# Filler matmuls that read the constant identity, with another set of the planner's numbers, in an attention and feed-forward kernel

## Chip, cores and metric

The kernel runs on one core of a Trainium2 chip. The metric is the device time in microseconds, the median of the runs shown; a lower time is better. Engines are named as in the profile: PE (TensorE) with PEld for its weight loads, DVE (VectorE), ACT (ScalarE), POOL (GpSimd), and SP, which issues most of the transfers.

## What is computed

For 4 batches and 8 heads with 576 positions of width 64, the reference computes causal softmax attention and a linear memory read, mixes them per head, and puts the result through a feed-forward layer:

```python
scores = np.where(causal, -1e9, scale * q @ k.T)
local = softmax(scores) @ v
mem_out = (phi(q) @ M_prev) / (phi(q) @ z_prev + 1e-6)   # phi(x) = (x if x > 0 else exp(x) - 1) + 1
x = g * mem_out + (1 - g) * local                        # g = sigmoid(beta), per head
r = np.maximum(x @ w_in, 0.0)                            # 2304 x 512 by 512 x 2048
out = (s * r * r + b) @ w_out                            # 2304 x 2048 by 2048 x 512
```

Both weights come as 64-bit floats and are converted on the chip.

## The kernel before

The work has two phases. The first, up to some 300 us, holds the attention of 16 pairs of heads (g = 0 to 15, pair p of batch b), the conversion of w_in, and the first feed-forward product for all rows of the first two batches and part of the third. The second holds the rest of that product, the conversion of w_out and the second product.

A pair goes through these steps. PE computes scores from qk into two PSUM tiles sb (L383). DVE adds the mask and takes the row minimum of the negated scores (L390) into P, which frees sb. ACT takes the exponential with row sums (L396). DVE turns the sums into 1/sum (L435, L436), and DVE or POOL scales P (L402). Beside this the memory part runs: a max (L319 on ACT, L321 on DVE or L323 on POOL), an exponential (L324), L325 on DVE, a product with z (L329), a sum (L331), L332 and a reciprocal (L335) on DVE, and a product that is put beside the scores in P (L342). PE transposes P in four groups, which the code calls banks, against the constant ident into four PSUM tiles tb (L463). ACT or DVE copies them out, to pt (L472) and F (L474, L476, L479). PE multiplies them with V, which holds v and the memory matrix (L514). The result is split into a high and a low part: ACT copies the high part (L535) and DVE subtracts (L536) into xs or x4, which gives the PSUM tile back.

The conversion of w_in goes in 20 pieces. Each piece uses one raw buffer xa of three and one work buffer of two, w0 and w1 (WT in the code). ACT starts it (L560), three DVE steps follow on the same buffer (L561, L562, L564), then the high part is made on ACT or POOL (L569, L567) and the low part on DVE or POOL (L571, L573). The first product (L580 to L582) takes xs or x4 and both parts.

No scheduler of the framework orders the first phase. The class `Plan` (L44) holds every step with an engine, an estimated cost, a rank, what it reads and writes, and which PSUM tile it takes and gives back. Its function `deal` places the steps in time by these estimates, lowest rank first among those that can go, and the program is written out in that order. Semaphores are put in from what each instruction really reads and writes. The tables from L292 on are its inputs: per pair, which engine takes the max (RELU), the copies (COPY, one letter for each of four banks) and the scalings (SCAL, one letter for each of five row blocks), when a pair is due (AT), and offsets for ranks (UC for copies, UX for the splits, RPS and RQS for the memory part). HIGH and LOW give the engine for the two parts of each piece of w_in.

After all steps are placed, `waits` (L157) goes over PE's steps. Where the plan shows PE idle for longer than two fillers and a margin, and a PSUM tile is free over that gap, it puts in filler matmuls. They are written by `warm`: 128 columns of `busy` against themselves. `busy` is no constant: it is the first 128 columns of the work buffer w0, cleared once at the start.

```python
busy = WT[0][:, :128]                                                        # L268
plan.idle = "TS", 0.3, lambda n, pool, k: warm(n, TB[k] if pool == "T" else SB[k])   # L291
raw, w = RAWS[n % 3][:, :n_], WT[n % 2][:, :n_]                              # L547
```

Of the kernel before, what the change touches and what calls it, by code (L numbers as in the profile page):

```python
# [43 lines left out]
class Plan:  # L44
# [6 lines left out]
    RATE = 220.0e3  # L51
    SWITCH = {"full": 0.22, "row": 0.13, "col": 0.13}
    TURN = 110
    HOLD, WORK, WAIT = (2.5, 3), (1, 5), (0.15, 0.05)
    FREE = {"DVE": 0.05, "POOL": 0.10}

    def __init__(self, **pools):
# [4 lines left out]
    def add(self, eng, cost, fn, rank, reads=(), writes=(), take=(), give=(), bytes=0, mode=None, slack=0.0, port=False):  # L62
        s = dict(eng=eng, cost=cost, fn=fn, rank=rank, take=take, give=give, bytes=bytes, mode=mode, slack=slack, port=port or eng == "POOL",
                 n=len(self.steps), out=[], end=None)
        deps = {self.wrote[k]["n"]: self.wrote[k] for k in (*reads, *writes) if k in self.wrote}
        for k in writes:
            deps |= {r["n"]: r for r in self.read.pop(k, ())}
            self.wrote[k] = s
        for k in reads:
            self.read.setdefault(k, []).append(s)  # L70
        s["need"] = len(deps)
        s["deps"] = list(deps.values())
        for d in s["deps"]:
            d["out"].append(s)
        self.steps.append(s)
        return s
# [95 lines left out]
def attention_moe_kernel(  # L172
# [15 lines left out]
    nc = tc.nc  # L188
# [16 lines left out]
    ident = const.tile([128, 128], F32, name="ident")  # L205
# [36 lines left out]
    SB = [ps_a.tile([128, 1024], F32, name=f"sb{k}") for k in range(2)]  # L242
    TB = [ps_a.tile([128, 512], F32, name=f"tb{k}") for k in range(4)]
# [23 lines left out]

    busy = WT[0][:, :128]  # L268

    def warm(n, ps):  # L270
        for _ in range(n):
            nc.tensor.matmul(ps[:, :128], lhsT=busy, rhs=busy, start=True, stop=True)

    def setup():
        nc.vector.memset(busy, 0.0)
        nc.vector.memset(omg, 0.0)
        warm(WARM, TB[3])
        nc.gpsimd.memset(mask, 0.0)
        for r, c in ((slice(0, 128), slice(448, 576)), (slice(0, 64), slice(576, 640)), (slice(64, 128), slice(576, 640))):
            nc.gpsimd.affine_select(  # L280
                out=mask[r, c], in_=mask[r, c], pattern=[[-1, c.stop - c.start]],
                compare_op=ALU.is_ge, fill=NEG, base=0, channel_multiplier=1,
            )
        for t in SM:
            nc.gpsimd.memset(t, 1e-9)
# [2 lines left out]
    same = lambda x: x  # L288

    plan = Plan(S=2, T=4)  # L290
    plan.idle = "TS", 0.3, lambda n, pool, k: warm(n, TB[k] if pool == "T" else SB[k])  # L291
    WARM, FILL = 7, (0, 0, 0, 0)  # L292
    UR, UC, UX = 1.5, 2, 1
    RP, RC, RT, RA, RX = 0.7, 0.5, 1.4, 2.0, 2.6
    RPS = [0.6, 0.9, -0.5, 0.6, 0.6, 0.6, 0.2, 0.6, ] + [-2] * 8
    RQS = [0, -1.5, 0.5, -1, 0.9, -1, 0.7, 0.3, ] + [0.9] * 8
    RSR, WL = 0.6, 5
    RELU = "APAAADPAADAAAAAA"
    ZMUL = "PPPDDDDDDPPPPPPP"
    PUTS = "PPPDPPPPDDPPPPPP"  # L300
    COPY = ["AADD", "DAAD", "AAAD", "AAAA", "AAAA", "AAAA", "AAAA", "AAAD", "DDAD", "AAAD", ] + ["AAAD"] * 6
    SCAL = ["PPPPP", "PPPPP", "DPPPP", "DDDDD", "DPPPP", "PPPDD", "DPPPD", "DDDDD", "DPPPD", "PPPDD", ] + ["PPPPP"] * 6
    HIGH, LOW = "AAPAAAAAPPAAAPAPPPAA", "DPPDDPDPDDPDDDDDPDDD"
    PARTS = "3232332223222222"
    AT = [-1.4, 0.9, 5.1, 7.8, 12.2, 13.1, 15.5, 19.7, 24.3, 26.2, 29.8, 31.5, 47.5, 23.2, 53.5, 29.1]
    W0, W1, W2, W3, WA, WB, WC, WD, WS = 4.5, 6.3, 6, 4, 8, 10, 14, 0.4, 0.6

    def phi(g):
        b, p = divmod(g, NP)
        u, r0 = g % 2, AT[g]  # L310
        q, z, n, P = QS_[u], ZS[u], NRM[u], PR[u]
# [5 lines left out]
            writes=[("z", u)], bytes=65536)  # L317
        if RELU[g] == "A":
            add("ACT", 0.72, lambda: nc.scalar.activation(PHR, q, AF.Relu), r0 + RPS[g], [("q", u)], ["phr"])  # L319
        elif RELU[g] == "D":  # L320
            add("DVE", 0.45, lambda: nc.vector.tensor_scalar(PHR, q, 0.0, None, ALU.max), r0 + RPS[g], [("q", u)], ["phr"], port=True)  # L321
        else:
            add("POOL", 0.88, lambda: nc.gpsimd.tensor_scalar(PHR, q, 0.0, None, ALU.max), r0 + RPS[g], [("q", u)], ["phr"])  # L323
        add("ACT", 0.72, lambda: nc.scalar.activation(q, q, AF.Exp), r0 + RPS[g] + 0.01, [], [("q", u)])  # L324
        add("DVE", 0.73, lambda: nc.vector.scalar_tensor_tensor(q, q, 1.0, PHR, ALU.min, ALU.add), r0 + RPS[g] + 0.1,  # L325
            ["phr"], [("q", u)], port=True)
        side = lambda c: (("POOL", nc.gpsimd), ("DVE", nc.vector))[c == "D"]
        ez, mul = side(ZMUL[g])
        add(ez, 1.54 if ez == "POOL" else 0.83, lambda: mul.tensor_mul(  # L329
            PHR, q, z.unsqueeze(1).to_broadcast([128, 5, 2, D])), r0 + RQS[g] + 0.01, [("q", u), ("z", u)], ["phr"], port=True)  # L330
        add("DVE", 0.73, lambda: nc.vector.tensor_reduce(n, PHR, AX.X, ALU.add), r0 + RQS[g] + 0.02, ["phr"], [("n", u)])  # L331
        add("DVE", 0.08, lambda: nc.vector.scalar_tensor_tensor(  # L332
            n, n, 1e-6, gin[:, hp:hp + 2].unsqueeze(1).unsqueeze(3).to_broadcast([128, 5, 2, 1]), ALU.add, ALU.mult),
            r0 + RQS[g] + 0.03, ["gin"], [("n", u)], port=True)
        add("DVE", 0.13, lambda: nc.vector.reciprocal(n, n), r0 + RQS[g] + 0.04, [], [("n", u)])  # L335

# [17 lines left out]
    def attention(g):  # L354
        b, p = divmod(g, NP)
        u, r0 = g % 2, AT[g]
        own = g >= NP
# [48 lines left out]
        for v, group in enumerate(visits):  # L406
# [60 lines left out]
        def copy(put, k, h, ps):  # L467
            t = TB[ps[h]]
            hs = slice(64 * h, 64 * h + 64)
            half = lambda a: a.rearrange("p j (r c) -> p j r c", c=128)[:, :, :, hs]  # L470
            if k < 2:
                put(pt[:, :, :, 128 * k:128 * k + 128][:, :, :, hs], t.rearrange("p (j r c) -> p j r c", j=2, c=64))  # L472
            elif k == 2:
                put(half(F[:, :, 320:832]), t.rearrange("p (j r c) -> p j r c", j=2, c=64))  # L474
            elif h:
                put(F[:, :, 0:384].rearrange("p j (r c) -> p j r c", c=128)[:, :, :, 0:64],  # L476
                    t[:, 0:384].rearrange("p (j r c) -> p j r c", j=2, c=64))
            else:
                put(half(F[:, :, 64:320]), t[:, 0:256].rearrange("p (j r c) -> p j r c", j=2, c=64))  # L479

        join = JOIN[g]
        some = [((0, 3),) if join in "ac" else ((0,), (3,)), ((1, 2),) if join in "bc" else ((1,), (2,))]
# [8 lines left out]
        for q, k in enumerate((0, 3, 1, 2)):  # L491
            ps = PS[k]
            r = r0 + RT + 0.1 * q
            for h in range(2):
                cost = dict(A=0.48 if k < 3 else 0.30 + 0.13 * h, D=0.58 if k < 3 else 0.33 + 0.13 * h)
                c = COPY[g][k]
                add(dict(A="ACT", D="DVE")[c], cost[c], lambda k=k, h=h, ps=ps: copy(
                    dict(A=nc.scalar.copy, D=nc.vector.tensor_copy)[COPY[g][k]], k, h, ps), r + 0.1 - UC,
                    [("tp", g, k)], [("pt", u if k > 1 else 2, h, k)], give=[(ps, h, "T")])
# [90 lines left out]
    def first(m, b, f, EARLY):  # L590
        ps = []
        pool = HOME[m]
        part = lambda: TB[ps[0]] if pool == "T" else SB[ps[0]][:, :CM]
# [28 lines left out]
            tick()  # L622

    LEFT = 7
    HOME = "TTTTTTTTTSTTTTTTTTTTTSSSSSTTSSSTSTTSSSTSS"
    JOIN = "b0b00000b0caa0bb"
    EARLY = 1
    MM = [(b, f) for b in range(B - 1) for f in range(NF - LEFT * (b == 2))]
    WRANK = [W0, W1, W2, W3] + [WA + WD * k for k in range(4)] + [WB + WD * k for k in range(4)] + [
# [259 lines left out]
    for t in range(NPT):  # L889
        if t == 0:  # L890
            g_load(1)
        for i, m in enumerate(SEQ):
            n = 7 * t + i + AH
# [3 lines left out]
            n = i if t else i - 2  # L897
# [55 lines left out]
```

## Time and profile before

| | before |
|---|---|
| runs | 556.72, 556.23, 555.96 us, median 556.23 |
| profiled execution | 556.89 us, span 555.1 us |
| PE busy | 540.1 us, 97% of the span |
| DVE, ACT, POOL busy | 398.4, 400.6, 258.2 us |
| granted clock, mean | 0.991 |
| chain that ended last | PE 89%, DVE 6%, ACT 3%, POOL 1% |
| calls of the filler | 39, seven of them at the very start |

The span is 1.8 us shorter than the time of the same execution, and that execution is 0.66 us above the median. PE is nearly always busy and holds most of the chain, so the places to read are those where it is not: the page's slices show PE under nine tenths in the first seventy microseconds, and a granted clock of six tenths in one of them. A call of the filler on 32-bit data is two records in the trace. Idle time in front of a group stands with what ended it, and the chain tells whether that wait mattered for the end.

### The profile page before, as it was taken

What the parts mean: (1) busy time and instruction counts of PE and PEld (TensorE: products, weight loads), DVE (VectorE), ACT (ScalarE), POOL (GpSimd) and SP (SyncE); (2) the same over time, 40 slices, a digit from 0 to 9 for tenths busy, and PEclk for the clock granted to TensorE, in tenths of its full rate; (3) what the DMA queues carried; (4) which work ended last, traced back from release to release, by engine and by line L of the source; (5) the groups of instructions that cost most, each with busy time, mean ns of one, the idle gap of its engine ahead of it and who ended that gap; (6) DMA issues with size and microseconds to landing.
All of it is one profiled execution on the core that took longest, in us unless ns stands there. A gap on an engine that the chain in (4) does not pass through costs nothing.

```text
span 555.1 us, 11449 instructions
## 1 busy us (share of the span) xinstructions
PE 540.1 (97%) x4086; PEld 445.9 (80%) x4086; DVE 398.4 (72%) x976; ACT 400.6 (72%) x878; POOL 258.2 (47%) x273
## 2 busy tenths in 40 slices
PE   8988799999999999999999999999999999999997
PEld 6756577777777777777778888889999999999996
DVE  5998799999896643324219969334888898888872
ACT  6887789876688963666435668959987977987840
POOL 4971256331445861442400000327578669668760
PEclk9999699999999999999999999999999999999999
DMA  6645566735535443221157564538425435353101
GB/s 198 182 141 176 156 204 213 243 125 159 178 108 162 123 127 122 78 86 63 58 180 312 190 239 157 190 125 289 142 87 155 140 112 165 105 153 122 39 30 38
DMA packets 56665, 81.50 MB, mean 147 GB/s; under 512 B 7584, under 2 KB 39072, under 8 KB 56608
## 3 DMA queue, kind: packets, MB, share of 16 engines
q1 hardware_dynamic: 54064, 78.63, 44.0%
q10 hardware_dynamic: 2544, 2.14, 1.1%
q8 instruction: 32, 0.52, 0.4%
q14 instruction: 25, 0.20, 0.1%
HBM read 57.15 MB, written 23.59 MB: 145 GB/s over the span
## 4 chain that ended last, share of the span: by engine, by line
PE 89%; DVE 6%; ACT 3%; POOL 1%; issue 1%; DVEq 0%; ACTq 0%; POOLq 0%
PE yps L808 12%; PE yps L812 11%; PE sb L514 7%; PE sb L383 6%; PE hps L580 5%; PE hps L581 5%; PE hps L582 5%; PE tb L580 5%; PE yps L811 5%; PE yps L810 5%; PE tb L463 4%; PE tb L581 4%; PE tb L582 4%; PE sb L580 3%; PE sb L582 2%; PE sb L581 2%
## 5 line engine op out<-in xcount | busy, mean ns | idle before, releaser
L396 ACT ACTIVATE P<-P,mn 128x448 f32<-128x448 f32 (+4 forms) x160 | 88.4, 561 | 25.9 <-DVE mn L390 24.8
L402 POOL TENSOR_SCALAR P<-P,sr,omg 128x192 f32<-128x192 f32 (+4 forms) x120 | 76.5, 654 | 64.9 <-DVE sr L436 45.2
L812 PE MATMUL yps<-rb,op 128*128 128x256 f32 x360 | 101.1, 281 | 0.0
L390 DVE CUSTOM_DVE_ANT_0 P<-sb,mask 128x448 f32<-128x448 f32 (+4 forms) x160 | 70.8, 481 | 21.7 <-PE sb L383 21.5
L808 PE MATMUL yps<-rb,op 128*128 128x512 f32 x216 | 76.9, 396 | 0.0
L812 PEld LDWEIGHTS yps<-rb,op 128*128 128x128 f32 x360 | 67.9, 189 | 0.0
L383 PE MATMUL sb<-qk 64*128 64x288 f32 (+4 forms) x384 | 58.5, 420 | 1.1 <-DVE mn L390 0.8
L788 POOL TENSOR_TENSOR sum<-src 128x512 f32<-128x512 f32 x10 | 13.0, 1298 | 90.9 <-ACT src L772 76.2
L796 POOL TENSOR_TENSOR op<-src,op 128x512 fp32r<-128x512 f32 x30 | 43.8, 1480 | 20.0 <-ACT op L795 19.9
L819 DVE TENSOR_TENSOR yu<-yu,yps 128x256 f32<-128x256 f32 x90 | 36.5, 413 | 20.1 <-PE yps L812 19.1
L383 PEld LDWEIGHTS sb<-qk 64*128 64x128 f32 x384 | 36.4, 194 | 15.4 <-issue 5.3
L463 PEld LDWEIGHTS tb<-ident,P 64*128 64x128 f32 x928 | 36.7, 142 | 14.3 <-issue 4.2
L808 PEld LDWEIGHTS yps<-rb,op 128*128 128x128 f32 x216 | 40.6, 188 | 9.0
L463 PE MATMUL tb<-ident,P 64*128 64x64 f32 x928 | 41.2, 230 | 5.5 <-DVE P L402 2.4
L810 PE MATMUL yps<-rb,op 128*128 128x256 f32 x144 | 40.5, 281 | 0.0
L811 PE MATMUL yps<-rb,op 128*128 128x256 f32 x144 | 40.5, 281 | 0.0
L795 ACT CAST op<-src 128x512 fp32r<-128x512 f32 x50 | 30.4, 615 | 12.1 <-PE yps L812 10.6
L796 DVE TENSOR_TENSOR op<-sum,op 128x512 fp32r<-128x512 f32 x36 | 38.8, 1078 | 0.2
L472 ACT COPY pt<-tb 128x512 f32<-128x512 f32 x58 | 31.1, 588 | 9.9 <-PE tb L463 5.2
L796 POOL TENSOR_TENSOR op<-w1H,op 128x512 fp32r<-128x512 f32 x24 | 35.0, 1483 | 0.0
L587 ACT ACTIVATE r<-hps 128x256 f32<-128x256 f32 x62 | 21.9, 382 | 16.3 <-DMA r_d<-r 12.1
L396 ACT ACTIVATION_READ_ACCUMULATOR P<-P,mn 128x1 f32 x160 | 31.5, 197 | 0.0
(172 smaller groups left out, 1549.7 us busy)
## 6 DMA issues: line engine op xcount, KB each, us to landing
r_d<-r SPq DMA_DIRECT2D x41, 256.0 KB, 2.3
src<-r_d SPq DMA_DIRECT2D x20, 512.0 KB, 4.7
qk<-in_qk_t_dram SPq DMA_DIRECT2D x15, 576.0 KB, 4.3
raw<-in_moe_w_out_dram SPq DMA_DIRECT2D x16, 512.0 KB, 7.1
w1H<-r_d SPq DMA_DIRECT2D x16, 512.0 KB, 4.4
xa<-in_moe_w_in_dram SPq DMA_DIRECT2D x12, 512.0 KB, 4.4
r_d<-r SPq DMA_DIRECT2D x48, 128.0 KB, 1.8
qs<-in_q_rows_dram SPq DMA_DIRECT2D x16, 320.0 KB, 4.0
```

The source lines that it names most:

```text
L383: nc.tensor.matmul(at(ps, j, o, n), lhsT=qk[rs, 128 * i:128 * i + 128], rhs=qk[rs, S + 64 + c0:S + 64 + c0 + n], start=True, stop=True, ti ...
L390: nc.vector.tensor_tensor_reduce(P[:, j, PB[i] + 64:PB[i] + 64 + n], at(ps, j, o, n), m, -SCALE, 3.0e38, ALU.add, ALU.min, mn[:, j, i:i + 1])
L396: nc.scalar.activation(pt, pt, AF.Exp, scale=-1.0, bias=mn[:, j, i:i + 1], accum_out=sm[:, j, i, 0:1])
L402: e.tensor_scalar(pt, pt, sr[:, j, i:i + 1], omg[:, h:h + 1], ALU.mult, ALU.mult)
L463: nc.tensor.transpose(TB[ps[h]][:, o[h]:o[h] + 64], P[rs, j, c:c + 128], ident[rs, rs], tile_position=(64 * h, 0))
L580: nc.tensor.matmul(ps, lhsT=wH[:, p, fs], rhs=xs[:, 0], start=p == 0, stop=False)
L581: nc.tensor.matmul(ps, lhsT=wH[:, p, fs], rhs=xs[:, 1], start=False, stop=False)
L796: (nc.gpsimd if m in ONPOOL else nc.vector).tensor_sub(L, x, H.bitcast(F32))
L808: nc.tensor.matmul(tile, lhsT=H, rhs=B, start=f == 0, stop=False)
L810: nc.tensor.matmul(ps, lhsT=H, rhs=B[:, 0], start=f == 0, stop=False)
L811: nc.tensor.matmul(ps, lhsT=H, rhs=B[:, 1], start=False, stop=False)
L812: nc.tensor.matmul(ps, lhsT=L, rhs=B[:, 0], start=False, stop=f == KF - 1)
```

## The change

The fillers that `waits` puts in read `ident` where they read `busy`; the seven at the start keep `busy`. With that come other values in the planner's tables: the margin for staying in a PE mode, UC, UX, RT, RA, RPS, RQS, WL, RELU, COPY, SCAL, HIGH, LOW, AT, W3, HOME and JOIN. Nothing that is computed changes.

```diff
@@ class Plan
-    HOLD, WORK, WAIT = (2.5, 3), (1, 5), (0.15, 0.05)
+    HOLD, WORK, WAIT = (2.5, 3), (1, 5), (0.05, 0.05)
@@ fillers
-    def warm(n, ps):
+    def warm(n, ps, some=busy):
         for _ in range(n):
-            nc.tensor.matmul(ps[:, :128], lhsT=busy, rhs=busy, start=True, stop=True)
+            nc.tensor.matmul(ps[:, :128], lhsT=some, rhs=some, start=True, stop=True)
...
-    plan.idle = "TS", 0.3, lambda n, pool, k: warm(n, TB[k] if pool == "T" else SB[k])
+    plan.idle = "TS", 0.3, lambda n, pool, k: warm(n, TB[k] if pool == "T" else SB[k], ident)
...
-    UR, UC, UX = 1.5, 2, 1
-    RP, RC, RT, RA, RX = 0.7, 0.5, 1.4, 2.0, 2.6
+    UR, UC, UX = 1.5, 1, 2
+    RP, RC, RT, RA, RX = 0.7, 0.5, 1.2, 2.6, 2.6
...
-    RELU = "APAAADPAADAAAAAA"
+    RELU = "AAPAADPAADAAAAAA"
...
-    COPY = ["AADD", "DAAD", "AAAD", "AAAA", "AAAA", "AAAA", "AAAA", "AAAD", "DDAD", "AAAD", ] + ["AAAD"] * 6
-    SCAL = ["PPPPP", "PPPPP", "DPPPP", "DDDDD", "DPPPP", "PPPDD", "DPPPD", "DDDDD", "DPPPD", "PPPDD", ] + ["PPPPP"] * 6
-    HIGH, LOW = "AAPAAAAAPPAAAPAPPPAA", "DPPDDPDPDDPDDDDDPDDD"
+    COPY = ["ADAD", "DAAD", "AAAD", "AAAA", "AAAA", "AAAA", "AAAA", "AAAD", "DDAD", "DAAD", ] + ["AAAD"] * 6
+    SCAL = ["PPPPP", "PPPPP", "DPPPP", "DDDDD", "DPPPP", "PPPDD", "PPPDD", "DDDDD", "PPPDD", "PPDDD", ] + ["PPPPP"] * 6
+    HIGH, LOW = "AAPAPAAAPPAAPPAAPAPA", "DPPDDPDPDDPDDDDDDPDP"
...
-    AT = [-1.4, 0.9, 5.1, 7.8, 12.2, 13.1, 15.5, 19.7, 24.3, 26.2, 29.8, 31.5, 47.5, 23.2, 53.5, 29.1]
+    AT = [0.6, 1.5, 4.8, 7.8, 11.7, 13.1, 15.5, 20.1, 24.5, 26.2, 31.1, 32.1, 47.5, 27.5, 54.0, 32.0]
...
```

The order on DVE in the middle of the conversion of the third piece of w_in (w0) and the fourth (w1), with the splits of pair 2 between; in brackets which engine or queue each waits for. Before:

```order
L562 SCALAR_TENSOR_TENSOR w0_106<-xa1_104,w0_106 128x256 [waits DMAHW4_49,DVE_49]
L562 SCALAR_TENSOR_TENSOR w1_107<-xa2_105,w1_107 128x256 [waits DMAHW3_49,DVE_49]
L536 TENSOR_TENSOR x4_141<-tb1_99,x4_141 128x64 [waits PE_49,Activation_49]
L564 SCALAR_TENSOR_TENSOR w0_106<-xa1_104,w0_106 128x256 [waits DVE_49,PE_49]
L536 TENSOR_TENSOR xs_135<-tb1_99,xs_135 128x256
```

and with the change:

```order
L562 SCALAR_TENSOR_TENSOR w0_106<-xa1_104,w0_106 128x256 [waits DMAHW4_49,DVE_49]
L562 SCALAR_TENSOR_TENSOR w1_107<-xa2_105,w1_107 128x256 [waits DMAHW3_49,DVE_49]
L536 TENSOR_TENSOR x4_141<-tb2_100,x4_141 128x64 [waits PE_49,Activation_49]
L564 SCALAR_TENSOR_TENSOR w0_106<-xa1_104,w0_106 128x256 [waits DVE_49]
L536 TENSOR_TENSOR xs_135<-tb2_100,xs_135 128x256
```

The steps stand in the same order; L564 no longer waits for PE.

The same place on PE: the end of the product with V of pair 2, the fillers, the first transposes of pair 3. Before:

```order
L514 MATMUL tb3_101<-F0_127,V0_125 64x256 x2
L514 MATMUL tb3_101<-pt_129,V0_125 64x256 x6
L514 MATMUL tb3_101<-F0_127,V0_125 64x128 x2
L272 MATMUL tb2_100<-w0_106 128x128 [waits DVE_49]
L272 MATMUL tb2_100<-w0_106 128x128 x7
L463 MATMUL tb2_100<-ident_65,P1_124 128x64
```

and with the change:

```order
L514 MATMUL tb1_99<-F0_127,V0_125 64x256 x2
L514 MATMUL tb1_99<-pt_129,V0_125 64x256 x6
L514 MATMUL tb1_99<-F0_127,V0_125 64x128 x2
L272 MATMUL tb3_101<-ident_65 128x128 x8
L463 MATMUL tb3_101<-ident_65,P1_124 128x64 [waits DVE_49]
```

The eight fillers stay where they were and wait for nothing; the wait for DVE stands at the first transpose.

DVE between the last reductions of pair 1 (P1) and the first of pair 2 (P0, sb1). Before:

```order
L435 TENSOR_REDUCE sr1_122<-sm1_120 128x2x4 [waits Activation_49]
L325 SCALAR_TENSOR_TENSOR qs1_114<-qs1_114,phr_108 128x640 [waits Activation_49]
L436 RECIPROCAL sr1_122<-sr1_122 128x2x4 [waits DVE_49]
L474 COPY F0_127<-tb0_98 128x2x4x64 [waits PE_49]
L474 COPY F0_127<-tb1_99 128x2x4x64 [waits PE_49]
L435 TENSOR_REDUCE sr1_122<-sm1_120 128x2 [waits Activation_49]
L436 RECIPROCAL sr1_122<-sr1_122 128x2 [waits DVE_49]
L479 COPY F0_127<-tb0_98 128x2x2x64 [waits PE_49]
L476 COPY F0_127<-tb2_100 128x2x3x64 [waits PE_49,Activation_49]
L331 TENSOR_REDUCE nrm1_116<-phr_108 128x10 [waits Pool_49]
L390 ISA P0_123,mn0_117<-sb1_97,mask_102 128x448 [waits PE_49]
```

and with the change:

```order
L479 COPY F0_127<-tb2_100 128x2x2x64 [waits PE_49]
L476 COPY F0_127<-tb3_101 128x2x3x64 [waits PE_49]
L435 TENSOR_REDUCE sr1_122<-sm1_120 128x2x4 [waits Activation_49]
L436 RECIPROCAL sr1_122<-sr1_122 128x2x4 [waits DVE_49]
L435 TENSOR_REDUCE sr1_122<-sm1_120 128x2 [waits Activation_49]
L436 RECIPROCAL sr1_122<-sr1_122 128x2 [waits DVE_49]
L472 COPY pt_129<-tb0_98 128x8x64 [waits PE_49]
L472 COPY pt_129<-tb1_99 128x8x64 [waits PE_49]
L325 SCALAR_TENSOR_TENSOR qs1_114<-qs1_114,phr_108 128x640 [waits Activation_49]
L390 ISA P0_123,mn0_117<-sb1_97,mask_102 128x448 [waits PE_49]
```

L325 has moved behind the copies, the two L474 have gone to ACT and two L472 have come, and L331 has moved further down. Later on DVE, L335 of pair 1 stood ahead of the first L561 and now stands right behind it. On POOL the two L342 of pair 0 have moved ahead of its two 576-wide L402, and five L402 of pair 1 ahead of its L329.

## Rows read from the trace of the kernel before

**Rows 1.** Busy time of each engine in four stages, with granted clock and DMA share.

```profile
10.00:34.00 24.00, 21.32 (x238) 15.54 (x237) 22.68 (x76) 20.06 (x61) 20.49 (x27) 1.00 0.62 193
52.00:68.00 16.00, 11.49 (x98) 8.86 (x100) 11.43 (x40) 9.45 (x27) 3.28 (x4) 0.68 0.50 158
68.00:140.00 72.00, 72.00 (x606) 54.25 (x604) 70.71 (x202) 59.66 (x153) 28.42 (x35) 1.00 0.58 186
140.00:230.00 90.00, 89.68 (x775) 68.03 (x772) 53.12 (x186) 63.26 (x171) 48.52 (x67) 1.00 0.41 131
```

The columns are the stretch and its length, then PE, PEld, DVE, ACT and POOL busy with their records, the granted clock, DMA share, GB/s.

**Rows 2.** Chain that ended last, 51 to 55 us: start, length, what.

```profile
52.32 2.07 PE tb L272 x16
...
54.41 0.43 DVE w L564
```

**Rows 3.** Timeline of DVE, 52 to 64 us: start, length, instruction, idle before.

```profile
52.52 0.22 DVE L536 TENSOR_TENSOR x<-tb,x 128x64 fp32r<-128x64 f32 x1
54.41 0.43 DVE L564 SCALAR_TENSOR_TENSOR w<-xa,w 128x256 uint32<-128x256 uint32 x1 [1.68 <-PE tb L272]
...
60.68 0.29 DVE L561 TENSOR_SCALAR w<-w 128x256 uint32<-128x256 uint32 x1 [1.07 <-PE tb L272]
...
63.34 0.35 DVE L390 CUSTOM_DVE_ANT_0 P<-sb,mask 128x192 f32<-128x192 f32 x1
```

**Rows 4.** Timeline of PE, 58 to 67 us.

```profile
58.55 0.87 PE L463 MATMUL tb<-ident,P 64*128 64x64 f32 x10 [1.76 <-DVE P L402]
...
64.79 2.24 PE L383 MATMUL sb<-qk 64*128 64x288 f32 x8
66.95 0.83 PE L514 MATMUL tb<-F,V 128*64 128x320 f32 x4
```

**Rows 5.** Timeline of DVE, 17 to 41 us.

```profile
17.14 0.22 DVE L335 RECIPROCAL nrm<-nrm 128x10 f32<-128x10 f32 x1
...
19.67 1.24 DVE L325 SCALAR_TENSOR_TENSOR qs<-qs,phr 128x640 f32<-128x640 f32 x1 [0.33 <-ACT qs L324]
...
23.15 0.81 DVE L331 TENSOR_REDUCE nrm<-phr 128x10 f32<-128x640 f32 x1
...
27.07 2.10 DVE L561 TENSOR_SCALAR w<-w 128x256 uint32<-128x256 uint32 x1
...
40.35 0.28 DVE L561 TENSOR_SCALAR w<-w 128x256 uint32<-128x256 uint32 x1
```

**Rows 6.** Timeline of POOL, 15 to 36 us.

```profile
15.46 1.63 POOL L402 TENSOR_SCALAR P<-P,sr,omg 128x576 f32<-128x576 f32 x2
...
18.83 1.41 POOL L342 TENSOR_TENSOR P<-qs,nrm 128x384 f32<-128x384 f32 x2
...
22.52 5.12 POOL L402 TENSOR_SCALAR P<-P,sr,omg 128x448 f32<-128x448 f32 x9
27.61 1.41 POOL L342 TENSOR_TENSOR P<-qs,nrm 128x384 f32<-128x384 f32 x2
...
34.45 1.68 POOL L329 TENSOR_TENSOR phr<-qs,z 128x640 f32<-128x640 f32 x1 [3.20 <-DVE qs L325]
```

**Rows 7.** Groups of DVE's instructions by shape, 66 to 230 us: busy, mean ns, idle before.

```profile
L402 DVE TENSOR_SCALAR P<-P,sr,omg 128x448 f32<-128x448 f32 x6 | 4.3, 722 | 0.0
L402 DVE TENSOR_SCALAR P<-P,sr,omg 128x64 f32<-128x64 f32 x8 | 2.6, 351 | 0.0
L472 DVE COPY pt<-tb 128x512 f32<-128x512 f32 x4 | 2.5, 675 | 0.0
L402 DVE TENSOR_SCALAR P<-P,sr,omg 128x320 f32<-128x320 f32 x2 | 1.4, 722 | 0.0
```

**Rows 8.** Busy time by engine, 57 to 67 us (columns as in rows 1).

```profile
57.00:67.00 10.00, 7.31 (x60) 5.58 (x60) 7.17 (x27) 7.11 (x19) 2.09 (x3) 0.50 0.47 153
```

**Rows 9.** Timelines of DVE and of PE, 112 to 117 us.

```profile
112.77 1.65 DVE L402 TENSOR_SCALAR P<-P,sr,omg 128x576 f32<-128x576 f32 x2
...
116.48 0.71 PE L463 MATMUL tb<-ident,P 64*128 64x64 f32 x16
```

More of the change, by code (lines that the diff above doesn't have):

```diff
@@ L290, in attention_moe_kernel @@
     plan = Plan(S=2, T=4)
-    plan.idle = "TS", 0.3, lambda n, pool, k: warm(n, TB[k] if pool == "T" else SB[k])
+    plan.idle = "TS", 0.3, lambda n, pool, k: warm(n, TB[k] if pool == "T" else SB[k], ident)
     WARM, FILL = 7, (0, 0, 0, 0)
-    UR, UC, UX = 1.5, 2, 1
-    RP, RC, RT, RA, RX = 0.7, 0.5, 1.4, 2.0, 2.6
-    RPS = [0.6, 0.9, -0.5, 0.6, 0.6, 0.6, 0.2, 0.6, ] + [-2] * 8
-    RQS = [0, -1.5, 0.5, -1, 0.9, -1, 0.7, 0.3, ] + [0.9] * 8
-    RSR, WL = 0.6, 5
-    RELU = "APAAADPAADAAAAAA"
+    UR, UC, UX = 1.5, 1, 2
+    RP, RC, RT, RA, RX = 0.7, 0.5, 1.2, 2.6, 2.6
+    RPS = [0.6, 0.9, 0, 0.6, 0.6, 0.6, 0, 0.4, ] + [-2] * 8
+    RQS = [0.7, -1, 0.9, -1, 0.9, 0.5, 0.5, 0, ] + [0.7] * 8
+    RSR, WL = 0.6, 3
+    RELU = "AAPAADPAADAAAAAA"
     ZMUL = "PPPDDDDDDPPPPPPP"
     PUTS = "PPPDPPPPDDPPPPPP"
-    COPY = ["AADD", "DAAD", "AAAD", "AAAA", "AAAA", "AAAA", "AAAA", "AAAD", "DDAD", "AAAD", ] + ["AAAD"] * 6
-    SCAL = ["PPPPP", "PPPPP", "DPPPP", "DDDDD", "DPPPP", "PPPDD", "DPPPD", "DDDDD", "DPPPD", "PPPDD", ] + ["PPPPP"] * 6
-    HIGH, LOW = "AAPAAAAAPPAAAPAPPPAA", "DPPDDPDPDDPDDDDDPDDD"
+    COPY = ["ADAD", "DAAD", "AAAD", "AAAA", "AAAA", "AAAA", "AAAA", "AAAD", "DDAD", "DAAD", ] + ["AAAD"] * 6
+    SCAL = ["PPPPP", "PPPPP", "DPPPP", "DDDDD", "DPPPP", "PPPDD", "PPPDD", "DDDDD", "PPPDD", "PPDDD", ] + ["PPPPP"] * 6
+    HIGH, LOW = "AAPAPAAAPPAAPPAAPAPA", "DPPDDPDPDDPDDDDDDPDP"
     PARTS = "3232332223222222"
-    AT = [-1.4, 0.9, 5.1, 7.8, 12.2, 13.1, 15.5, 19.7, 24.3, 26.2, 29.8, 31.5, 47.5, 23.2, 53.5, 29.1]
-    W0, W1, W2, W3, WA, WB, WC, WD, WS = 4.5, 6.3, 6, 4, 8, 10, 14, 0.4, 0.6
+    AT = [0.6, 1.5, 4.8, 7.8, 11.7, 13.1, 15.5, 20.1, 24.5, 26.2, 31.1, 32.1, 47.5, 27.5, 54.0, 32.0]
+    W0, W1, W2, W3, WA, WB, WC, WD, WS = 4.5, 6.3, 6, 5, 8, 10, 14, 0.4, 0.6
     def phi(g):
@@ L624, in attention_moe_kernel @@
     LEFT = 7
-    HOME = "TTTTTTTTTSTTTTTTTTTTTSSSSSTTSSSTSTTSSSTSS"
-    JOIN = "b0b00000b0caa0bb"
+    HOME = "TTTTTTTTTSTTTTTTTTTTTSTSSSTTSSSTSTTSSSTSS"
+    JOIN = "b0b00000b000a0bb"
     EARLY = 1
```

## The prediction

> **What bounds the kernel now.** I read the table by stage first, for one question: in which stages is TensorE (PE) not full. From 68 us to 230 it is busy 72.00 of 72 us and 89.68 of 90, and VectorE (DVE) beside it 70.71 of 72 in the first of these [rows 1]. So from 68 us on the time is a fixed amount of PE work, and an edit pays only by letting that dense part begin earlier, or costs by tearing it open. The stages that are not full are 10 to 34 us (21.32 of 24) and above all 52 to 68 us (11.49 of 16), where the mean granted clock is 0.68 as well [rows 1].
>
> Then I read what ends the waits in 52 to 68. The chain that ended last shows a piece that computes nothing: 16 records of the filler line L272, 2.07 us, between two DVE steps on the conversion buffer w [rows 2]. In DVE's timeline the second of these, L564, sits idle 1.68 us until PE's L272 is done; 6 us later L561 waits 1.07 us for the same reason [rows 3]. That is a knot: the fillers read w0, so they wait for the step that writes it, and the next step on w0 waits for the fillers, with DVE's whole queue behind it: the xs copies that give PSUM back, and the scalings L402 that the next transposes need.
>
> **The change part by part.**
>
> *The fillers read the identity.* The order on both engines shows L564 without its wait on PE, at the same place, and the eight fillers without a wait. L564 then follows the L536 before it (52.52 and 0.22 [rows 3]) at about 52.7 us instead of 54.41; everything from L571 to the last L402 moves up with it, and so do the transposes at 58.55 us [rows 4]. That is **-1.7 us** on the path. The fillers themselves start when the PV product ends and use time in which PE has nothing else. The 1.07 us at L561 I cost at nothing: the scores of 64.79 us wait for PE's own transposes and fillers, while DVE had finished the last reduction that gives their PSUM back at about 63.7 us (63.34 and 0.35) [rows 3, 4]. If PE gets over 1.1 us faster there, that cover is gone and the 1.07 us counts too.
>
> *Fewer fillers.* 39 calls become 35, two records each: 8 records at about 0.13 us (2.07 over 16 [rows 2]) make 1.0 us less PE work, all of it in waits that end with another engine: 0. Bounds: 0 and -1.0.
>
> *The new order between 17 and 34 us.* In the old order DVE's L325 of pair g=1 starts at 19.67 us, and the plain shift L561 takes 2.10 us at 27.07, against 0.28 for the same shape at 40.35 [rows 5]. During those 2 us POOL runs the end of L402 and both L342 [rows 6], so 1.8 us is blocking, not work. In the new order L325 stands behind the copies F and two L472 of pair 0. Walk: L335 ends at 17.4 us [rows 5]; POOL now runs the L342 pair (1.41) ahead of the two 576-wide L402 (1.63) [rows 6], so these end near 20.3; the transposes that need them give the first L472 at about 21.0, L325 ends at 23.1 with both copies before it (0.675 each [rows 7]) and its own 0.8, or at 23.5 if POOL blocks it as at 19.67. That is 2.2 to 2.6 us later than before (19.67 and 1.24). POOL fills the gap with five of the nine L402 that made 5.12 us (some 2.9 us) [rows 6], so the L342 pair of g=1 starts near 27.9 instead of 27.61. From the L331 at 23.15 to L561 DVE needs 3.9 us [rows 5], and the same steps now follow L325, so it comes to L561 near 27.2; L335, for which that L342 pair waits, now stands behind L561, so POOL itself has to stop and let it through: it ends near 28.2 instead of 29.1, and 0.2 goes to L335. Taken: **-0.7 us**, passed on because DVE is nearly full until 52 us. Bounds: -1.8, if nothing blocks L561; +2.6, if POOL does idle in front of the late L329. I take a value near the first since POOL's work is moved, not added: the max of pair 2 (L323), which it gets in place of pair 1's, falls before the 3.20 us in which it idled until 34.45 [rows 6].
>
> The Trainium skill, SBUF — State Buffer, section Who interferes with whom, says that VectorE and GpSimd hold a shared pair of ports as an exclusive lock for one instruction at a time. By that L561 should have lost only the rest of one L402, some 0.5 us; here it lost 1.8 over three POOL instructions, so the trace is harsher than the page [rows 5, 6]. Going by the page for the new order, L561 loses less still and the term would be about -1.1; the total would move by 0.4 us.
>
> *The clock.* The granted clock is 0.50 from 57 to 67 us, with 7.31 us of PE work in it [rows 8]; before it fell PE had run only the fillers, then transposes with idle time between. That pattern stays. Bounds: the fall does not come, half of 7.31, -3.7; the clock rises at the same moment as now, and the PV product that began at 66.95 us [rows 4] slides 2.4 us into the slow part and returns half of that, +1.2. With the low-work part shifted whole, I take 0.
>
> *After 68 us.* Tables for later pairs give DVE four L402 of 448, two of 320 and two L472 more, and four L402 of 64 less: 4 x 0.722 + 2 x 0.722 + 2 x 0.675 - 4 x 0.351 = 4.3 us [rows 7]; one L571 leaves for POOL, uncounted. Of these only the pair for g=6 (two times 0.37) lies in 68 to 140, where DVE has 1.3 us free; the rest falls after 140, where it is busy 53.12 of 90 [rows 1]. PE is not waiting at the closest place I found: L402 ends at 114.4 and its transposes run at 116.48 [rows 9]. Taken: 0. If the cover is gone: 4.3 - 1.3 = +3.0.
>
> Sum: -1.7 - 0.7 = -2.4. On the profiled execution (556.89 us, span 555.1) that is 554.5; the median of the runs is 0.66 lower, so the median becomes **553.8 us**.
>
> **The rivals.**
>
> *No slow clock.* The stretch is shorter by 1.7 us and PE idles less in it, so the clock may stay up or recover early. Then 2.4 + 3.7 is saved: 550.1. Against it: between the PV products only short transposes and fewer fillers are left. Chance 0.17.
>
> *Given back.* The knot goes, but the PV product runs slow (+1.2) and the reorder yields nothing (+0.7): -0.5, 555.7. For it: the clock stayed down 10 us whatever PE did at its end. Chance 0.20, with the case that DVE's extra 4.3 us lands where it is full (-2.4 + 3.0, 556.8).
>
> *Slower: the clock falls a second time, near 20 us.* Three fillers that stood between the transposes there are gone, and TensorE now waits for the two L402 that POOL runs later; a stretch of transposes and idle time is what came before the fall at 57. If it falls for 10 us, PE has 21.32/24 x 10 = 8.9 us of work at half speed; with half of it hidden behind DVE, +4.4: 556.23 - 2.4 + 4.4 = 558.2. It decides as soon as a granted clock under 1 shows between 18 and 32 us. Against it: score products stand close on either side. Chance 0.12.
>
> *The change does not do what it says* can be excluded as to the waits (the order shows them gone), not as to their worth: that is the second rival.
>
> **How the numbers follow.** The forecast (a gain of 1.3 to 4 us) has 0.51, the rivals 0.17, 0.20, 0.12. About 0.2% (1.1 us) is what a measurement here can tell from no change. Faster by more: 0.51 + 0.17 = 0.68; within: 0.20; slower: 0.12. The range leaves out the far half of the first rival and most of the last: **551.0 to 557.2**; the forecast's own range is 552.3 to 555.0.
>
> **What would show it.** Right: no wait of DVE on L272; L564 of piece n=2 about 2.4 us earlier than 54.41, the scores at 64.79 by as much or more; a short L561 near 27 us; PE full from 66 us on, with no wait over 0.3. Wrong: the fillers still on the chain as a wait of DVE; a clock under 1 near 20 us; PE waiting for L402, L472 or L571 between 68 and 165 us; or a slow-clock stretch longer than 10 us.

## The result and the profile after

| | before | after |
|---|---|---|
| runs beside each other | median 556.70 us (6 runs, 555.96 to 557.85) | median 551.76 us (6 runs, 551.01 to 552.63) |
| profiled execution, span | 556.89, 555.1 us | 551.01, 549.2 us |
| mean granted clock | 0.991 | 0.997 |

The ratio is 0.9910, with a 95% interval of 0.9894 to 0.9926: 4.9 us faster, where 2.4 were forecast. The value lies in the range given (551.0 to 557.2), near its lower end, and 0.5 us under the forecast's own range (552.3 to 555.0). The profiled execution of after is the fastest of its six, so the two traces lie 5.9 us apart, one more than the medians. After's six runs differ by 1.6 us, and most of that goes with the mean granted clock: they are 551.0 to 551.3 at 0.996 or 0.997 and 552.2 to 552.6 at 0.993 or 0.994.

The stages of after, to be held against [rows 1], and the window of [rows 8]:

```profile
10.00:34.00 24.00, 21.95 (x243) 15.47 (x244) 22.68 (x79) 20.57 (x61) 21.07 (x27) 1.00 0.59 192
52.00:68.00 16.00, 13.64 (x130) 10.09 (x130) 15.79 (x54) 13.12 (x37) 6.46 (x10) 0.89 0.69 216
68.00:140.00 72.00, 71.68 (x598) 54.00 (x598) 69.48 (x196) 59.71 (x154) 31.02 (x37) 1.00 0.61 191
140.00:230.00 90.00, 89.93 (x791) 68.17 (x789) 53.51 (x184) 58.98 (x161) 43.68 (x62) 1.00 0.39 121
...
57.00:67.00 10.00, 10.00 (x98) 7.05 (x97) 9.79 (x35) 8.60 (x27) 4.58 (x6) 0.91 0.65 208
```

From 68 us on PE is as full as it was to within some 0.3 us, so what the new tables moved to DVE there costs nothing that shows. All of the gain is made before. In 52 to 68 PE has 13.64 us instead of 11.49, DVE 15.79 instead of 11.43, and the mean clock is 0.89 instead of 0.68: it stands at 0.50 (1.2 GHz) for some 3.4 us in this execution, from about 55.5, where before it did so from 56.9 to 67.1.

PE's timeline of after, the places of [rows 2, 4]:

```profile
49.85 2.05 PE L272 MATMUL tb<-ident 128*128 128x128 f32 x16
...
55.33 0.79 PE L463 MATMUL tb<-ident,P 64*128 64x64 f32 x10 [1.72 <-DVE P L402]
...
59.72 1.19 PE L383 MATMUL sb<-qk 64*128 64x288 f32 x8
60.84 0.76 PE L514 MATMUL tb<-F,V 128*64 128x320 f32 x4
```

and DVE's, the places of [rows 3] and [rows 5]:

```profile
21.60 1.08 DVE L325 SCALAR_TENSOR_TENSOR qs<-qs,phr 128x640 f32<-128x640 f32 x1
...
27.26 0.28 DVE L561 TENSOR_SCALAR w<-w 128x256 uint32<-128x256 uint32 x1
...
31.67 0.70 DVE L562 SCALAR_TENSOR_TENSOR w<-xa,w 128x256 uint32<-128x256 uint32 x1
32.29 1.33 DVE L325 SCALAR_TENSOR_TENSOR qs<-qs,phr 128x640 f32<-128x640 f32 x1
...
51.25 0.41 DVE L564 SCALAR_TENSOR_TENSOR w<-xa,w 128x256 uint32<-128x256 uint32 x1
...
56.31 0.28 DVE L561 TENSOR_SCALAR w<-w 128x256 uint32<-128x256 uint32 x1
```

No step of DVE waits for L272 any more. The lead of after grows along the way: L564 3.2 us (54.41 to 51.25), the transposes 3.2 (58.55 to 55.33), the scores 5.1 (64.79 to 59.72), the next product with V (the PV product) 6.1 (66.95 to 60.84), the span 5.9. So there are two questions: why 3.2 and not 2.4 up to the transposes, and where the 2.9 behind them come from.

### The profile page after: what moved, and what is told of

It is laid out like the page before. It is cut to its first block, busy times and chain, and to the rows that moved or that the text cites. A ratio compares the mean times of both kernels' runs of the same rounds, so it can differ in the third digit from the quotient of the medians.

```text
span 549.2 us, 11418 instructions
## 1 busy us (share of the span) xinstructions
PE 537.4 (98%) x4078; PEld 443.5 (81%) x4078; DVE 396.5 (72%) x979; ACT 397.7 (72%) x875; POOL 259.6 (47%) x273
## 4 chain that ended last, share of the span: by engine, by line
PE 85%; DVE 8%; ACT 2%; POOL 1%; DMA 1%; issue 1%; DVEq 0%; ACTq 0%; POOLq 0%
PE yps L808 12%; PE yps L812 11%; PE sb L514 7%; PE sb L383 6%; PE hps L580 5%; PE hps L581 5%; PE hps L582 5%; PE yps L811 5%; PE yps L810 5%; PE tb L463 4%; PE tb L580 4%; PE tb L581 3%; PE tb L582 3%; DVE P L390 3%; PE sb L580 3%; PE sb L581 2%
## 5 line engine op out<-in xcount | busy, mean ns | idle before, releaser
L402 POOL TENSOR_SCALAR P<-P,sr,omg 128x192 f32<-128x192 f32 (+4 forms) x118 | 75.9, 657 | 66.2 <-DVE sr L436 41.4
L390 DVE CUSTOM_DVE_ANT_0 P<-sb,mask 128x448 f32<-128x448 f32 (+4 forms) x160 | 71.1, 483 | 17.7 <-PE sb L383 17.6
L463 PE MATMUL tb<-ident,P 64*128 64x64 f32 x928 | 42.3, 228 | 4.4 <-DVE P L402 2.4
L796 DVE TENSOR_TENSOR op<-sum,op 128x512 fp32r<-128x512 f32 x36 | 37.7, 1048 | 0.3 <-ACT op L795 0.2
L472 ACT COPY pt<-tb 128x512 f32<-128x512 f32 x54 | 29.0, 586 | 12.2 <-PE tb L463 7.8
```

What stands on the lines that cost most here:

```text
L390: nc.vector.tensor_tensor_reduce(P[:, j, PB[i] + 64:PB[i] + 64 + n], at(ps, j, o, n), m, -SCALE, 3.0e38, ALU.add, ALU.min, mn[:, j, i:i + 1])
L463: nc.tensor.transpose(TB[ps[h]][:, o[h]:o[h] + 64], P[rs, j, c:c + 128], ident[rs, rs], tile_position=(64 * h, 0))
L796: (nc.gpsimd if m in ONPOOL else nc.vector).tensor_sub(L, x, H.bitcast(F32))
```

## The experiments

My theory after the result: the fillers on w0 tied more than one knot, the end of these waits is most of the gain, the rest is the slow clock that ends sooner, and the new tables add little. The rivals: the tables did it; one knot did it and turned the clock; the fillers themselves were the cost. In the kernels marked with a star below one line stands more above the loops, so that their L562 is L561 of the others, L563 is L562, L565 is L564, and so on.

**Fillers and tables apart.** Fillers on the identity, tables of before:

```diff
 # kernel before
-    plan.idle = "TS", 0.3, lambda n, pool, k: warm(n, TB[k] if pool == "T" else SB[k])
+    plan.idle = "TS", 0.3, lambda n, pool, k: warm(n, TB[k] if pool == "T" else SB[k], ident)
```

> The tables of the kernel before; only the fillers that the planner puts in read the identity, as in the changed kernel. Nothing else moves. Theory (the knot is 1.7 us, and what ends the slow clock early is that the scores behind the knot come sooner): L564 of w0 starts at about 52.7 us instead of 54.41, without a wait on L272; the PV product of g=3 comes more than 1.7 us earlier than 66.95; the time falls by 1.7 to 4.6 us. Rival A (the knot only moves: the clock stays low for its 10 us): the time falls by 1.2 to 1.8 us and a window from 55 to 66 us shows 0.50 throughout. Rival B (the tables did everything): within 0.6 us of the kernel before.

552.89 us against 556.68 beside it; ratio 0.993 (0.9916 to 0.9945), which is -3.9 us. Its PE, DVE's L564, and its clock in steps of 2 us:

```profile
56.06 0.56 PE L463 MATMUL tb<-ident,P 64*128 64x64 f32 x10 [1.72 <-DVE P L402]
...
60.11 1.60 PE L383 MATMUL sb<-qk 64*128 64x288 f32 x8
61.64 0.76 PE L514 MATMUL tb<-F,V 128*64 128x320 f32 x4
```

```profile
51.98 0.41 DVE L564 SCALAR_TENSOR_TENSOR w<-xa,w 128x256 uint32<-128x256 uint32 x1
```

```profile
54.00:56.00 2.00, 0.28 (x2) 0.14 (x2) 2.00 (x7) 1.51 (x4) 0.72 (x1) 1.00 0.86 230
56.00:58.00 2.00, 1.94 (x30) 1.71 (x30) 2.00 (x9) 1.88 (x7) 0.00 (x0) 0.87 0.66 255
58.00:60.00 2.00, 2.00 (x22) 1.73 (x20) 2.00 (x11) 1.88 (x6) 0.00 (x0) 0.50 0.04 14
60.00:62.00 2.00, 2.00 (x18) 1.36 (x18) 1.86 (x8) 1.73 (x5) 0.94 (x1) 0.78 0.83 252
```

The transposes are 2.5 us earlier than before, the scores 4.7, the PV product 5.3. Here 1.7 were forecast, and in this execution the slow stretch is already the short one. The six runs fall in two groups: three at a mean clock of 0.996 took 551.5 to 552.6 us, three at 0.990, no higher than before's 0.991, took 553.2 to 553.7. So some 3.3 us of the gain come with no more clock than before had, and some 1.5 more where the clock is better; where the clock is low in the three runs at 0.990 no trace shows. The theory holds, and rivals A and B fall: the interval (3.1 to 4.7 us) holds neither's band.

The changed kernel with the fillers back on w0:

```diff
 # kernel after
-    plan.idle = "TS", 0.3, lambda n, pool, k: warm(n, TB[k] if pool == "T" else SB[k], ident)
+    plan.idle = "TS", 0.3, lambda n, pool, k: warm(n, TB[k] if pool == "T" else SB[k])
```

> The changed kernel with its tables; the planned fillers read the conversion buffer w0 again, as before. Theory: the early gain stays (PV of g=2 at about 46.6 us instead of 47.97), and the knot is back: L564 waits about 1.7 us for L272 near 51 us, and the slow stretch of the clock is 8 to 10 us long again; the time lies 1.0 to 2.0 us under the kernel before. Rival A (early gains are given back at the knot): within 0.6 us of the kernel before. Rival B (the tables did everything, the fillers' data nothing): 4 to 5 us under the kernel before, like the changed kernel.

556.39 us; ratio 0.9997 (0.9987 to 1.0007). The knot is back (DVE's L564, first line), and PE's clock falls a second time, early (the stage, second line):

```profile
53.91 0.42 DVE L564 SCALAR_TENSOR_TENSOR w<-xa,w 128x256 uint32<-128x256 uint32 x1 [1.67 <-PE tb L272]
```

```profile
10.00:34.00 24.00, 22.70 (x242) 16.21 (x241) 22.23 (x77) 20.62 (x62) 21.82 (x28) 0.93 0.60 182
```

The tables alone are worth at most 0.7 us, less than the 1.0 that I expected. Rival A's band holds the value, but its mechanism doesn't show: in this profile the PV product of pair 2 leads by 0.5 us (47.47 for 47.97; 46.6 were expected), and the scores behind the knot still lead by 0.5 (64.30 for 64.79). The lead was small from the start. This profile has one of the two lowest mean clocks (0.988) of its eleven runs, so the early fall is likely not in all of them.

**The knots one by one.** The kernel before has nine planned groups of fillers. In each of three kernels (with the star) only some of them read the identity:

```diff
 # kernel before, here the group near 41 us; (6,) near 52 us; (7, 8) near 60 us
-    plan.idle = "TS", 0.3, lambda n, pool, k: warm(n, TB[k] if pool == "T" else SB[k])
+    calls = iter(range(99))
+    plan.idle = "TS", 0.3, lambda n, pool, k: warm(n, TB[k] if pool == "T" else SB[k], ident if next(calls) in (5,) else busy)
```

> The kernel before; of its nine planned groups of fillers only the one between the scores near 41 us reads the identity (three calls), the others still read w0. Theory: L562 at 41.72 us, 0.86 long behind a gap, was a knot too, worth 0.7 us: it starts at about 41.4 with 0.5, and everything up to the fillers at 52.32 comes 0.7 earlier; L564 near 54.41 and L561 near 60.68 keep their waits of 1.7 and 1.1. Time 0.5 to 1.0 us under the kernel before. Rival (the prediction, which saw no knot there): within 0.3 us of the kernel before.

> The kernel before; only the eight fillers behind the product of pair 2, near 52.3 us, read the identity. Theory and prediction agree on 1.7 us up to the transposes at 58.55; L561 keeps its 1.07. Theory (three knots in a row, the clock's part comes from all of them together): time 1.5 to 2.2 us under the kernel before, the slow stretch of the clock as long as before (about 10 us). Rival (this knot alone also ends the slow clock early): 3 us or more under the kernel before.

> The kernel before; only the two groups of two fillers among the transposes at 59.35 and 62.75 us read the identity. Theory: L561 at 60.68 loses its 1.07 us, the row minima behind it on DVE come earlier, so ACT's exponential at 61.15 and copy L472 at 61.65, and PE's wait of 1.14 on that copy shrinks; the scores of 64.79 start 1.0 to 1.5 us earlier and the time is 1.0 to 1.6 us under the kernel before. Rival (the prediction: covered, worth nothing): within 0.3 us of the kernel before.

| identity in the group | median, before beside it | ratio to before, 95% | us by the ratio |
|---|---|---|---|
| near 41 us | 556.58, 556.56 | 0.9991 (0.9981 to 1.0001) | -0.5 |
| near 52 us | 555.12, 556.56 | 0.9973 (0.9963 to 0.9984) | -1.5 |
| near 60 us | 554.85, 556.56 | 0.9964 (0.9950 to 0.9979) | -2.0 |
| all nine | 552.89, 556.68 | 0.9930 (0.9916 to 0.9945) | -3.9 |

The ratio is estimated over all runs of both and need not be that of the medians. By the ratios the three add up to the whole (0.5 + 1.5 + 2.0 = 4.0); by the medians they make 3.1 of 3.8, so the sum is known to about 1 us. The other five groups lie before 21 us, and no step of DVE waits for them. The group near 41 us alone isn't told from nothing, neither by its interval nor by its median, but its trace shows it. Before, L562 on w0 starts after a gap of 0.14 us and takes 0.86; with that one group on the identity it follows at once and takes 0.52 (second line), and the L390 behind it starts at 41.90 instead of 42.50. The fillers of 52.32 start at 51.92: 0.4 us earlier, where 0.7 was expected. L561's wait of 1.07 us doesn't stay as expected but shrinks to 0.41: the clock falls later there, and the two fillers that it waits for take 0.86 us instead of 1.22. (In that profile the clock falls once more, to 0.50 from about 32 to 35 us; what that takes back no run shows.)

```profile
41.72 0.86 DVE L562 SCALAR_TENSOR_TENSOR w<-xa,w 128x256 uint32<-128x256 uint32 x1
```

```profile
41.45 0.52 DVE L563 SCALAR_TENSOR_TENSOR w<-xa,w 128x256 uint32<-128x256 uint32 x1
```

The group near 52 us is worth about what was expected of it (1.5 to 2.2), and its L564, called L565 there, starts at 52.56 us without a wait, where the prediction had 52.7. The slow stretch, which was to stay at about 10 us, is already shorter in its profile (about 7 us), and L561's wait is 0.78 instead of 1.07. The group near 60 us is the surprise. PE's rows of before there, and of DVE the step on w0 that lies between:

```profile
60.50 1.11 PE L463 MATMUL tb<-ident,P 64*128 64x64 f32 x16
62.75 1.20 PE L272 MATMUL tb<-w 128*128 128x128 f32 x4 [1.14 <-ACT pt L472]
```

```profile
62.19 0.42 DVE L564 SCALAR_TENSOR_TENSOR w<-xa,w 128x256 uint32<-128x256 uint32 x1
```

Kernel with only that group on the identity, PE, and ACT's copy:

```profile
60.53 1.12 PE L464 MATMUL tb<-ident,P 64*128 64x64 f32 x16
61.58 1.22 PE L272 MATMUL tb<-ident 128*128 128x128 f32 x4
...
63.64 1.88 PE L384 MATMUL sb<-qk 64*128 64x288 f32 x8
```

```profile
61.68 1.07 ACT L473 COPY pt<-tb 128x512 f32<-128x512 f32 x2 [0.88 <-PE tb L464]
```

The profile puts the 1.14 us down to ACT's copy. It was not that: with the identity the fillers start at 61.58 us, before the copy begins, and the copy itself starts where it did (61.68 for 61.65). They had waited for L564 on w0 (62.19 and 0.42, so 62.61), and L564 was late since L561 ahead of it had waited 1.07 us for the fillers of 59.35 [rows 3]. Each group waited for DVE's step and the next step for the group: the knot stopped PE too, with its whole queue, and the scores come 1.15 us earlier (63.64 for 64.79). My expectation here had the right size at the scores (1.0 to 1.5), a little too little in the time (1.0 to 1.6, against 1.7 by the medians), and the wrong way: I thought of ACT's exponential and copy.

**What the fillers are for.** No planned fillers at all, with either set of tables:

```diff
 # kernel after, and likewise kernel before
-    plan.idle = "TS", 0.3, ...
+    plan.idle = "TS", 1000.0, ...
```

> The changed kernel with no planned fillers at all (the seven at the start stay). Theory (fillers that nobody waits for cost nothing, and they are what keeps TensorE busy in the gap at 50 us): the clock falls sooner or stays low longer between 50 and 66 us, and the time is 0.5 to 3 us above the changed kernel. Rival (fillers are worth nothing, only their wait was the cost): within 0.5 us of the changed kernel, with the slow stretch of the clock 3 to 4 us long as there.

> The kernel before with no planned fillers at all (the seven at the start stay), so that the knot goes without the identity. Theory (the knot is the wait for fillers, and fillers serve the clock): L564 no longer waits for PE, -1.7 us, but the clock falls no later and stays low as long as before or longer; the time is 0 to 2 us under the kernel before, and above that of the tables of before with fillers on the identity. Rival (fillers are worth nothing): the same time as with fillers on the identity, 1.7 to 4.6 us under the kernel before.

554.26 us (ratio 0.9958, 0.9945 to 0.9971) and 554.72 (0.9971, 0.9960 to 0.9982). Taking fillers away ends the knots as well, yet it is 1.8 us slower than fillers on the identity with the tables of before and 2.5 slower with those of after. Of the first (tables of after), two stages:

```profile
10.00:34.00 24.00, 21.10 (x206) 14.99 (x205) 20.36 (x75) 19.34 (x59) 20.42 (x27) 0.79 0.53 164
...
52.00:68.00 16.00, 11.17 (x102) 7.80 (x100) 15.53 (x55) 12.37 (x37) 3.64 (x5) 0.68 0.69 212
```

The clock is down for some 10 us in each, in the first of them where neither before nor after had it down. Both theories hold: fillers have a worth of their own, and the clock is what differs in the traces; only their wait was the cost.

**Is it the identity?** Tables of before, fillers on the first 128 columns of the attention mask:

```diff
 # kernel before
+    ... warm(n, TB[k] if pool == "T" else SB[k], mask[:, :128])
```

> The tables of the kernel before; the planned fillers read the first 128 columns of the attention mask, a constant that is all zeros there, in place of w0 and of the identity. Theory (all that matters is that nobody writes what the fillers read): the same as with fillers on the identity, 3.1 to 4.7 us under the kernel before, no wait of DVE on L272. Rival (the data in the fillers matters, for instance to the clock): 1 us or more away from that, with another slow stretch of the clock.

552.14 us beside 557.20; ratio 0.9914 (0.9899 to 0.9928); clock 0.89 in 52 to 68, as in after. That is 4.8 us by the ratio, a little above the range expected (3.1 to 4.7); the interval overlaps that of the identity, and the runs at the same mean clock agree (at 0.996: 551.7 to 552.5 with the mask, 551.5 to 552.6 with the identity). So of these two constants it doesn't matter which the fillers read; that nobody writes it does.

**Can the rest of the slow clock go?** One more group of fillers, where PE waits 1.72 us for L402 ahead of the transposes of 55.33 (star); in after's tables, and in those of before:

```diff
 # kernel after
-    plan.idle = "TS", 0.3, lambda n, pool, k: warm(n, TB[k] if pool == "T" else SB[k], ident)
+    sizes = iter((3, 2, 6, 0, 2, 0, 3, 8, 6, 2, 2))     # the second 6 is new; a smaller cost lets the planner see its gap
+    plan.idle = "TS", 0.2, lambda n, pool, k: warm(next(sizes), TB[k] if pool == "T" else SB[k], ident)
```

> The changed kernel with one more group of fillers: six calls on the identity between the transposes of pair 3, where TensorE waits 1.72 us for DVE's L402 near 54 us; all other groups as in the changed kernel. Theory (idle time there lets the clock fall at 55.7): the slow stretch comes later or not at all, and the time is 0.4 to 1.5 us under the changed kernel's 551.76. Rival A (the clock falls all the same): within 0.4 us of the changed kernel. Rival B (the fillers hold back the transposes): up to 0.5 us above it.

> The tables of the kernel before, fillers on the identity, and one more group of six calls between the transposes of pair 3 where TensorE waits for L402. Theory: granted clock 1.00 from 50 to 70 us; beside fillers on the identity alone (552.89) 0.5 to 2 us faster, and above the changed kernel with the same group by what the new tables are worth, 0.3 to 1.1 us. Rival A (the clock falls all the same, with this order): like 552.89. Rival B (the new tables are worth nothing): the same as the changed kernel with that group.

> The changed kernel itself, beside the next one on the same chip. Theory: 551.0 to 552.6, 4.5 to 5.3 us under the kernel before, in two groups by the mean granted clock (0.997 and 0.994), about 1.1 us apart.

> The changed kernel with six filler calls more in the gap at 54 us, once more, beside the changed kernel on the same chip. Theory (the slow stretch goes, but DVE then bounds this place): 0.3 to 1.2 us under the changed kernel, mean clock 0.999 or 1.0 in every run. Rival (no gain): medians within 0.3 us.

| kernel | this | before beside it | ratio, 95% | mean clock of its runs |
|---|---|---|---|---|
| after, group added | 550.95 | 556.56 | 0.9899 (0.9883 to 0.9915) | 0.999 to 1.000 |
| the same, again | 550.87 | 557.20 | 0.9891 (0.9876 to 0.9906) | 0.999 to 1.000 |
| after, beside it | 551.38 | 557.20 | 0.9900 (0.9885 to 0.9916) | 0.993 to 1.000 |
| before's tables, identity, group added | 551.48 | 557.20 | 0.9901 (0.9884 to 0.9917) | 0.999 to 1.000 |

Of the first, a stage, and one wait of PE:

```profile
52.00:68.00 16.00, 14.83 (x145) 10.80 (x144) 16.00 (x56) 13.09 (x37) 6.39 (x10) 1.00 0.73 225
```

```profile
59.82 1.24 PE L384 MATMUL sb<-qk 64*128 64x288 f32 x6 [0.34 <-DVE mn L391]
```

The slow stretch is gone in all 13 runs of the two kernels, and it yields little: 0.5 us beside after (550.87 for 551.38), with intervals that overlap. DVE is now busy 16.00 of 16 us there, and PE waits for its minima. It is the best version measured, by about that half microsecond. With before's tables the same group brings a little more: 551.48 us, for 552.14 with fillers on the mask beside it and 552.89 with fillers on the identity, which were measured at another time. The two groups expected of after's own runs did not show: 552.24 at 0.996, 551.54 at 0.993, 551.22 at 1.000, 550.75 at 0.997. The first of these has a slower start (last section).

Five pairs show what the tables are worth: 0.3 (fillers on w0, 556.39 for 556.68), 0.5 (no fillers, 554.26 for 554.72), 0.6 (group added, 550.87 for 551.48), 0.8 (551.38 for 552.14, on identity and mask) and 1.1 us (fillers on the identity, 551.76 for 552.89, measured at different times). Each alone is within its uncertainty; all have one sign.

## Why the prediction was right and where it was wrong

The measured gain is twice the forecast's 2.4 us. It lies in the stated range because that also covers the near half of the rival *no slow clock*, and the clock made up only a part of the difference. That the value fell inside is in part luck; the direction, and the knot as its main cause, are not.

*The fillers read the identity, -1.7.* The mechanism and this size were right: 1.5 us for that group alone (0.9 to 2.1 by its interval), and its L564 at 52.56 us for 52.7.

*The wait that I did not see.* L562 at 41.72 us was a knot as well. It showed as a gap of 0.14 us without a releaser and a long instruction; the list of waits names L272 for L564 and L561 only, and I went by that list. The DVE step L564 of 54.41 gained 2.4 us from the fillers alone (51.98): 1.7 are its own wait, and the other 0.7 come from here. With only this group on the identity 0.4 arrived at the next fillers, and the time alone doesn't show it.

*"The 1.07 us at L561 I cost at nothing": this step failed.* I argued that the scores wait for PE's own transposes and fillers and that DVE had done its part a microsecond before. The first half is true, and it was the point: those fillers themselves waited 1.14 us for L564, which stood behind L561. I had looked at who waits for DVE among the steps that compute and taken the fillers as work that PE does when it has nothing else. Worth: 2.0 us (1.2 to 2.8) for the group, 1.15 of them seen directly at the scores.

*The clock, "I take 0": also mis-sized.* In the profiled execution it ended sooner, after 3.4 us instead of 10.2. What a better clock gives back is seen within one kernel: the two groups of runs with fillers on the identity and before's tables lie 1.5 us apart. From the scores to the PV product it is 2.16 us before (64.79 to 66.95) and 1.12 after (59.72 to 60.84), one microsecond of this. So the term was about -1 to -1.5, between the bounds (-3.7 and +1.2), and the rival of a clock that recovers early was half right. That PE had less idle time ahead of the scores once the knot near 60 us was gone goes with it, and six fillers more in the gap ahead of it kept the clock up in all 13 runs; which idle time makes it fall was not shown one by one. Part of it is already in the 1.5 and 2.0 us of the single knots, whose profiles show some 7 us of slow clock: the terms don't simply add.

*The new order, -0.7.* Right in size (0.3 to 1.1 us in the five pairs; L564 at 51.25 for 51.98 in the traces), not in its way. L561 reached its place as the walk said (27.2; 27.26 measured), in part by luck: L325 ended at 22.7 us, not at 23.1 to 23.5, and DVE then waited 0.44 us for scores. There L561 wasn't held up at all, though POOL ran through it:

```profile
25.14 3.08 POOL L402 TENSOR_SCALAR P<-P,sr,omg 128x320 f32<-128x320 f32 x5
...
31.36 1.59 POOL L402 TENSOR_SCALAR P<-P,sr,omg 128x448 f32<-128x448 f32 x2
```

The blocking moved to L562 (0.70 for 0.41) and to L325 (1.33 for 0.81), 0.8 us of the 1.8 that L561 had lost [rows 5], both beside POOL's L402 at 31.36. The Trainium skill, SBUF — State Buffer, section Who interferes with whom, gives whichever of the two engines issues first the ports that they share, as an exclusive lock for one instruction; these smaller losses, each under the 0.8 us of one such L402, agree with it. The 1.8 us of before, over three POOL instructions, do not, and L561's 0.28 us amid POOL's L402 fits only if it fell between two of them, which the trace doesn't tell.

*After 68 us, 0.* Right: PE 71.68 of 72 and 89.93 of 90. *Fewer fillers, 0.* No run tells this apart. *The clock near 20 us*, the slower rival, did not come in after, but its mechanism exists: with these tables and fillers on w0 the early stage shows 0.93, without fillers 0.79.

In sum the forecast of -2.4 lacked 0.4 to 0.7 us for the first knot, about 1.2 for PE's own wait near 60 us, and 1 to 1.5 for the clock; measured, 2.5 were missing.

## What to carry to other kernels

Work that only keeps an engine warm must read what nobody writes, a constant, and write what nobody needs, here a free PSUM tile. If it reads a buffer in use, it ties its queue to every writer of that buffer, in both directions, so count all its groups, and the filler's own waits as well as the waits for it. The releaser that a profile names is the one that ended last before the start (here ACT's copy at 62.72 us, PE's start at 62.75), whether the instruction needs it or not: ask the program's order what it really waits for.

## What the runs showed of the hardware

A slow clock cost less here than its length suggests: an estimated 6.6 us more at 0.50 (a mean clock of 0.990 for 0.996 over 550 us: 0.006 x 550, and twice that since the level is one half) cost 1.5 us. Taking the last 3.4 us away gave about 0.5 with after's tables, where DVE was then busy for all of 52 to 68 us and PE waited for it, and 0.7 to 1.4 with before's, where some runs had a longer slow clock to lose.

Matmuls can also be slow where the granted clock is recorded as 1.00. In the second profile of after the scores at 7.04 us and the fillers at 8.83 ran at about half pace (1.86 and 1.65 us), where the kernel before has 1.02 for scores of the same shape (7.04) and 0.94 for the same number of filler records (7.99); the window from 5 to 10 us of that profile shows 1.00:

```profile
7.04 1.86 PE L383 MATMUL sb<-qk 64*128 64x448 f32 x4 [0.15 <-DVE mn L390]
8.83 1.65 PE L272 MATMUL tb<-ident 128*128 128x128 f32 x6
```

```profile
5.00:10.00 5.00, 4.85 (x19) 2.62 (x18) 3.16 (x19) 3.12 (x13) 0.14 (x1) 1.00 0.85 267
```

Everything behind came 1.35 us later than in the first profile (the first PV product at 25.58 for 24.23 us), and the span is 1.3 us longer (550.5 for 549.2). Whether the record or something other than the clock is behind it, and why the start differs from run to run, stays open.
